# Four tokens a partition for x of batches 0 and 1, and a new order of the work up to the second chunk of w_in

## The chip, the cores and the metric

The kernel runs on one core of one Trainium2 chip. The metric is the time of one execution on the device, in microseconds (us). Four executions of the kernel before took 694.12, 694.25, 694.48 and 695.06 us; the median is 694.36. All data is float32, and the core's engines work side by side, each through its own list of instructions in program order: TensorE (PE, matmuls and transposes into PSUM banks), VectorE (DVE), ScalarE (ACT), GpSimd (POOL, hardly used here) and SyncE (SP), which issues all DMAs. They wait for each other through semaphores.

## What is computed

```python
# x (8, 8, 512, 64), state (8, 8, 32, 64): batches, heads, tokens or states, D
scores = scale * np.matmul(x, state.transpose(0, 1, 3, 2))
a = softmax(scores)                    # over the 32 states; max subtracted, 1e-9 added to the sum
xread = np.matmul(a, state)
scores2 = scale * np.matmul(state, x.transpose(0, 1, 3, 2))
a2 = softmax(scores2)                  # over the 512 tokens
sread = np.matmul(a2, x)
t = np.concatenate([xread, sread], axis=2)         # per head: 512 tokens, then 32 states
h = t.transpose(0, 2, 1, 3).reshape(8 * 544, 512) @ w_in      # w_in (512, 2048)
g = h * (1.0 / (1.0 + np.exp(-1.702 * h)))
out = g @ w_out                                     # w_out (2048, 512)
```

The inputs w_in and w_out arrive as 64-bit numbers and are turned into float32 on the core.

## The kernel before

The program is written out by hand: each engine runs its instructions in the order in which the Python code emits them (`manual_schedule`), so the order of the calls below is the order of each engine's queue. There is no planner and there are no due times.

**Weights.** w_in and w_out come as 32 pieces of 512 KB, 16 of w_in (four chunks `c` of 512 columns, four row blocks `k`) and 16 of w_out. Each is a DMA of SP (L199) and then three steps, called a piece's mask, clamps and rounding. `mask` (L221, DVE) takes the exponent bits. `round_a`, called by `powers_to`, clamps them with two Relu activations on ACT (L232, L233). `round_b`, called by `round_to`, is four DVE operations: `fraction` (L239), the sign (L250), the low word (L253) and the product (L257). `round_to(n, ahead)` finishes all pieces before n and, after each sign, has the masks and clamps of the next pieces done, `ahead` of them. The prologue's position of each such call sets where clamps stand in ACT's queue.

**Attention of batches 0 and 1, the prologue (L1188 to L1300).** `load_x` puts x into SBUF with 128 tokens a chunk, one per partition, in four DMAs a batch (L155), each run being one token of one head, 256 bytes. For later batches it already takes four tokens a partition, in runs of 1 KB (L152). `att_state` transposes the state of a batch and copies it on ACT into `pairs` (L308, block diagonal over two heads) and `stT` (L310). `xT_chunk` transposes one chunk of 128 tokens, four pairs of heads (L318), and copies it out on ACT (L319). `x_scores` makes the scores of one chunk for all heads (L325) in a PSUM bank that two chunks share. `head_max`, `head_sub`, `head_exp` and `head_norm` are the softmax over states (L338, L342, L346, L352 to L358), and `head_back` transposes the result (L367) and copies it to `aT` (L368). `att_scores` makes the second scores (L375) through `by_state`, one bank for each of two groups g of heads. Their softmax comes much later: `att_s_max` (L395), `att_s_exp` (L414), `att_s_norm` with `s_norm` (L420 to L423, where batches 0 and 1 scale the whole result), then `att_eT` (L509), `att_sread` (L523, L529) and `att_srT` (L537).

**The up projection of batches 0 and 1.** `att_M(b, c)` multiplies chunk c of w_in, all four row blocks, with the state (L375) and copies the two results M on ACT (L481). `up_x(b, f)` is two matmuls of M with aT (L552), followed by a Gelu on ACT (L555) into g_room; 16 of them per batch. `psH`, `att_ps` and the four `bank_o` are the eight PSUM banks; the last two of `bank_o` are `held`, and two banks of psH are `apart`. A matmul that reuses a bank waits until the engine that reads the old content is done. `keep_warm` issues matmuls of zeros.

**What follows.** The products with w_out for batch 0 (L1402) run piece by piece with the rounding of w_out and sums on DVE (L1332), interleaved with the rest of up_x of batch 1 (bank `down_up`). Then batch after batch runs through two levels of Strassen products (L695, L744, L1105), and a last pass for the state rows (L594). This part is not touched, apart from the order of rows in the stores of batches 0 and 1.

The order around the change, as it stands (L1200 to L1234), begins:

```python
    att_state(0)
    keep_warm(2, bank_o[0])
    xT_chunk(0, 0)
    keep_warm(2, bank_o[0])
    xT_chunk(0, 1)
    x_scores(0, 0, held)
    xT_chunk(0, 2)
    x_scores(0, 1, held)
    head_max(0, 0, held)
    mask(2)
```

Of the kernel before, what the change touches and what calls it, by code (L numbers as in the profile page):

```python
# [20 lines left out]
def kernel(  # L21
# [50 lines left out]
    out_x = out.rearrange("(b t) n -> b t n", b=B)[:, :S].rearrange("b (c q) n -> b c q n", c=SCH)  # L72
    out_s = out.rearrange("(b t) n -> b t n", b=B)[:, S:]
    x_v = x.rearrange("b h (c q) d -> b c q h d", c=SCH)
# [42 lines left out]
    pairs = konst.tile([P, NPR, NG, Ns], FP32, name="pairs")  # L117
# [17 lines left out]
    xn, xsq, stn = {}, {}, {}  # L135

    def load_state(b):
        stn[b] = apool.tile([P, NG, D], FP32, tag="stn", name=f"stn_{b}", bufs=2)
        for g in range(NG):
            nc.sync.dma_start(stn[b][:, g], st_v[b, g])  # L140

    def load_x(b):
        if b == 1:
            xn[b] = sums[:, 0].rearrange("p (c h d) -> p c h d", c=SCH, h=H)
        else:
            xn[b] = xpool.tile([P, SCH, H, D], FP32, tag="xn", name=f"xn_{b}")
        if b > 1:

            xn[b] = xn[b].rearrange("p c h d -> p (c h d)").rearrange("p (h c d) -> p h c d", h=H, c=SCH)
            for i in range(NG):  # L150
                h = slice(NPR * i, NPR * (i + 1))
                nc.sync.dma_start(xn[b][:, h].rearrange("p h c d -> p h (c d)"), x_four[b, :, h])  # L152
            return
        for c in range(SCH):
            nc.sync.dma_start(xn[b][:, c], x_v[b, c])  # L155
# [16 lines left out]
    def x_heads(b, c, j):  # L172
        return xn[b][:, c, NG * j : NG * (j + 1)].rearrange("q g d -> q (g d)")
# [7 lines left out]
    raw, power, begun = {}, {}, {}  # L181
# [59 lines left out]

    def round_b(i, ahead, follows):


        if i not in begun:
            fraction(i)
        dst = begun.pop(i)
        lo, hi = words(i)
        sc = power.pop(i)
        nc.vector.scalar_tensor_tensor(sc, hi, -0x80000000, sc, ALU.bitwise_and, ALU.bitwise_or)  # L250
        powers_to(ahead)

        nc.vector.scalar_tensor_tensor(dst, lo, 2.0**-32, dst.bitcast(I32), ALU.mult, ALU.add)  # L253
        del raw[i]
        if follows and i + 1 in raw:
            fraction(i + 1)
        nc.vector.scalar_tensor_tensor(dst, dst, 2.0**-20, sc.bitcast(FP32), ALU.mult, ALU.mult)  # L257
# [43 lines left out]
    def att_state(b):  # L301
        ps = att_ps([P, P], f"stT_{b}")
        nc.tensor.transpose(ps, stn[b].rearrange("p g d -> p (g d)"), ident)
        if b < 2:

            for g in range(NG):
                rows = slice(D * g, D * (g + 1))
                nc.scalar.copy(pairs[rows, :, g], ps[rows].rearrange("p (j n) -> p j n", n=Ns))  # L308
        A[b]["stT"] = apool.tile([P, P], FP32, tag="stT", name=f"stT_{b}", bufs=2)
        nc.scalar.copy(A[b]["stT"], ps)  # L310

    def xT_chunk(b, c):

        if c == 0:
            A[b]["xT"] = apool.tile([P, NPR, S], FP32, tag="xT", name=f"xT_{b}")
        ps = att_ps([P, NPR, P], f"xT_{b}_{c}")
        for j in range(NPR):
            nc.tensor.transpose(ps[:, j], x_heads(b, c, j), ident)  # L318
        nc.scalar.copy(A[b]["xT"][:, :, P * c : P * (c + 1)], ps)  # L319

    def x_scores(b, c, banks):

        ps = banks[c // 2].rearrange("p (c g j n) -> p c g j n", c=2, g=NG, j=NPR)[:, c % 2]
        for j in range(NPR):
            nc.tensor.matmul(ps[:, :, j], A[b]["xT"][:, j, P * c : P * (c + 1)], pairs[:, j], start=True, stop=True)  # L325

    def head_views(b, i, banks):
        a = A[b]
        if "mx" not in a:
            a["e1"] = apool.tile([P, SCH, NG, NPR, Ns], FP32, tag="e1", name=f"e1_{b}")  # L330
            a["mx"] = apool.tile([P, NG, NB], FP32, tag="mx", name=f"mx_{b}").rearrange("p g i -> p (g i)")
        n = NG * NB // 2
        t = a["e1"].rearrange("p c g j n -> p (c g j) n")[:, n * i : n * (i + 1)]
        return banks[i].rearrange("p (i n) -> p i n", n=Ns), t, a["mx"][:, n * i : n * (i + 1)]

    def head_max(b, i, banks):
        ps, _, mx = head_views(b, i, banks)
        nc.vector.reduce_max(out=mx, in_=ps, axis=AX.X)  # L338

    def head_sub(b, i, banks):  # L340
        ps, t, mx = head_views(b, i, banks)
        nc.vector.tensor_tensor(out=t, in0=ps, in1=mx.to_broadcast((P, NG * NB // 2, Ns)), op=ALU.subtract)  # L342
# [5 lines left out]
    def head_norm(b):  # L348

        t = A[b]["e1"]  # L350
        sm = apool.tile([P, NS1], FP32, tag="sm", name=f"sm_{b}")
        nc.vector.reduce_sum(out=sm, in_=t.rearrange("p c g j n -> p (c g j) n"), axis=AX.X)  # L352
        nc.vector.tensor_scalar(sm, sm, eps, None, ALU.add)
        nc.vector.reciprocal(out=sm, in_=sm)
        sm = sm.rearrange("p (c g j) -> p c g j", c=SCH, g=NG)
        for g in range(NG):
            e = t[:, :, g]
            nc.vector.tensor_tensor(out=e, in0=e, in1=sm[:, :, g].to_broadcast((P, SCH, NPR, Ns)), op=ALU.mult)  # L358

    def head_back(b, g):  # L360

        a = A[b]
        if g == 0:
            a["aT"] = low[:, :NG] if b == 1 else apool.tile([P, NG, S], FP32, tag="aT", name=f"aT_{b}")
        ps = att_ps([P, SCH, P], f"aT_{b}_{g}")
        for c in range(SCH):
            nc.tensor.transpose(ps[:, c], a["e1"][:, c, g].rearrange("p j n -> p (j n)"), ident)  # L367
        nc.scalar.copy(a["aT"][:, g], ps.rearrange("p c q -> p (c q)"))  # L368
# [8 lines left out]
    def att_scores(b):  # L377
        a = A[b]
        a["s"] = bank_o[:NG] if b == 0 else bank_o[NG:]
        by_state(b, a["s"], lambda rows, j: a["xT"][rows, j])  # L380

    def att_blocks(b):

        a = A[b]
        t = apool.tile([P, NG, NB, Ns], FP32, tag="e1", name=f"e1_{b}")
        a["e1"] = t
        for g in range(NG):
            nc.vector.transpose(t[:, g].rearrange("p i n -> p (i n)"), a["s"][g])

# [27 lines left out]
    def s_norm(b, g):  # L417

        e, sm = A[b]["e2"][g]
        nc.vector.tensor_scalar(sm, sm, eps, None, ALU.add)  # L420
        nc.vector.reciprocal(out=sm, in_=sm)
        if b < 2:
            nc.vector.tensor_scalar(e, e, sm, None, ALU.mult)  # L423
# [88 lines left out]
    def att_sread(b):  # L512
# [3 lines left out]
        for g in range(NG):  # L516
            for c in range(SCH):
                for j in range(NPR):
                    st = slice(Ns * j, Ns * (j + 1))
                    e, v = a["eT"][:, g, c, st], xn[b][:, c, NG * j + g] if b < 2 else None  # L520
                    if b > 1:
                        e, v = a["eT"][:, g, j, Ns * c : Ns * (c + 1)], xn[b][:, NG * j + g, c]
                    nc.tensor.matmul(  # L523
                        ps[st, g], e, v,
                        start=(c == 0), stop=(c == SCH - 1),
                    )
        sr = apool.tile([P, P], FP32, tag="sr", name=f"sr_{b}", bufs=2)
        if b < 2:
            nc.scalar.copy(sr, ps.rearrange("p g d -> p (g d)"))  # L529
        else:  # L530
            for g in range(NG):
                nc.scalar.activation(out=sr[:, D * g : D * (g + 1)], in_=ps[:, g], func=AF.Copy, scale=a["e2"][g][1])
# [662 lines left out]
    keep_warm(16)  # L1195
# [6 lines left out]
    keep_warm(2, bank_o[0])  # L1202
    xT_chunk(0, 0)
    keep_warm(2, bank_o[0])
    xT_chunk(0, 1)
    x_scores(0, 0, held)
    xT_chunk(0, 2)
    x_scores(0, 1, held)
    head_max(0, 0, held)
    mask(2)  # L1210
    head_sub(0, 0, held)
    fraction(2)
    xT_chunk(0, 3)
    x_scores(0, 2, held)
    x_scores(0, 3, held)
    powers_to(3)
# [4 lines left out]
    xT_chunk(1, 0)  # L1221
    head_exp(0)
    xT_chunk(1, 1)
    x_scores(1, 0, apart)
    round_to(3, 0)
    mask(3)
    xT_chunk(1, 2)
    x_scores(1, 1, apart)
    powers_to(4)
    keep_warm(2, held[0])  # L1230
    xT_chunk(1, 3)
    head_norm(0)
    head_back(0, 0)
    x_scores(1, 2, apart)  # L1234
    head_back(0, 1)
    x_scores(1, 3, apart)
    keep_warm(3, held[0])
    round_to(NPR, 1)
    att_M(0, 0)
    mask(NPR + 1)  # L1240
    mask(NPR + 2)
# [6 lines left out]
    powers_to(NPR + 2)  # L1248
    up_x(0, 0, True)
    up_x(0, 1, True)  # L1250
    round_to(NPR + 1, 0)
    head_norm(1)
    up_x(0, 2)
    for g in range(NG):
        head_back(1, g)
    powers_to(NPR + 3)
    up_x(0, 3)

# [9 lines left out]
    for i in range(nper):  # L1268
        up_x(1, i, bank=held[i] if i < 2 else None)
        if i + 1 < nper:  # L1270
            round_to(done["b"] + 1, 2 if i == 0 else AHEAD)
    att_M(0, 1)
    att_scores(1)
    turn(0, 1, (1, 1), [1, 1, 1])
# [6 lines left out]
    att_s_max(0)  # L1281
    att_s_max(1)
# [8 lines left out]
    for b in (1, 0):  # L1291
        att_s_exp(b, room[:, NG * b : NG * (b + 1)])
    rounds(3)
    for b in (1, 0):
        att_s_norm(b)
# [25 lines left out]
    def out_of(b):  # L1321
        return lambda r, n: out_x[b, r, :, n].rearrange("r q n -> q r n")
# [264 lines left out]
```

## Time and profile before

One execution was profiled. Its numbers, with those that matter for what follows:

| | |
|---|---|
| median of four executions | 694.36 us |
| the profiled execution | 694.85 us |
| its span, from the first to the last instruction | 693.1 us |
| granted TensorE clock over the span | 0.998 |
| PE busy from 0 to 10, 10 to 20, 20 to 30, 30 to 40, 40 to 50 us | 8.57, 8.60, 9.72, 9.12, 8.95 us |
| DVE busy in the same stretches | 3.56, 7.41, 9.86, 8.99, 9.82 us |
| ACT busy in the same stretches | 5.49, 6.01, 7.78, 9.00, 8.29 us |
| first real transpose of x of batch 0 / of batch 1 | 8.37 / 17.13 us |
| first matmul of up_x | 27.27 us |
| SP's issues of x: batch 0 / batch 1 | 3.04 to 7.92 / 10.73 to 16.58 us |

A row of the timeline gives the start in us, the duration, the engine, the line, the operation, the tile written and the tiles read (`out<-in`), the shapes, how many instructions are merged (`xN`) and, in brackets, the idle time before it and what ended it. PE matmuls are pipelined and their ends are modelled, so the distance of two starts says more than a duration. A matmul of float32 data shows as two instructions. In a table of windows, the columns are busy time and number of instructions of PE, PE's weight loads (PEld), DVE, ACT and POOL, then PE's granted clock, the share of the DMA engines' time in use, and GB/s. The chain of waits is followed back from the last instruction to what released each step.

### The profile page before, as it was taken

The numbers are of one execution on the slowest core, as the hardware profiler recorded it, in microseconds if no ns is written. First come the engines' busy times: TensorE is split into PE (matmuls) and PEld (weight loads), VectorE is DVE, ScalarE is ACT, GpSimd is POOL, SyncE is SP. The second block draws the span as 40 slices with busy tenths as digits, with TensorE's granted clock in tenths as the row PEclk, the third lists the DMA queues.
The fourth block names the chain that finished last, engine by engine and source line by source line (L and its number), as shares of the span: only waits on it lengthen the run. The fifth ranks groups of instructions, "written<-read, shape, count | busy, mean of one in ns | idle before, by whom it ended". The sixth has DMA issues, their size and how long they took to land.

```text
span 693.1 us, 13666 instructions
## 1 busy us (share of the span) xinstructions
PE 682.5 (98%) x5376; PEld 583.5 (84%) x5377; DVE 560.6 (81%) x1074; ACT 324.0 (47%) x712; POOL 1.0 (0%) x9
## 2 busy tenths in 40 slices
PE   8999999999999999999999999999999999999996
PEld 4533587778999899889988999989988998999995
DVE  5999998999999887788969796888688895886540
ACT  5887843224346533753365435643366236421410
POOL 0000000000000000000000000000000000000000
PEclk9999999999999999999999999999999999999999
DMA  8921338056443564347441845166424740251001
GB/s 223 384 97 54 102 122 185 7 192 208 159 91 111 176 197 138 59 137 201 138 93 49 234 160 122 24 185 204 119 42 141 210 139 16 76 168 46 3 1 30
DMA packets 106320, 87.41 MB, mean 126 GB/s; under 512 B 64784, under 2 KB 85776, under 8 KB 106256
## 3 DMA queue, kind: packets, MB, share of 16 engines
q1 hardware_dynamic: 106256, 86.53, 42.9%
q8 instruction: 43, 0.70, 0.4%
q14 instruction: 21, 0.17, 0.1%
HBM read 68.94 MB, written 17.56 MB: 125 GB/s over the span
## 4 chain that ended last, share of the span: by engine, by line
PE 92%; ACT 2%; DMA 2%; DVE 1%; SPq 1%; issue 0%; DVEq 0%
PE low L695 28%; PE o L1105 15%; PE o L695 15%; PE upx L1105 6%; PE h L552 4%; PE o L1402 4%; PE M L375 4%; PE down L1402 3%; PE o L594 2%; PE upw L1105 2%; PE o L744 2%; PE down_up L552 2%; PE sr L523 1%; PE upx_sr L1105 1%; DMA out_dram<-osb_sr 1%; PE o L375 1%
## 5 line engine op out<-in xcount | busy, mean ns | idle before, releaser
L695 PE MATMUL low<-w_out,g_room 128*128 128x128 f32 x416 | 54.3, 276 | 0.0
L695 PEld LDWEIGHTS low<-w_out,g_room 128*128 128x128 f32 x416 | 50.5, 192 | 4.5 <-issue 4.2
L1105 PE MATMUL o<-ta,M 128*128 128x256 f32 x192 | 49.9, 382 | 0.0
L1105 PE MATMUL upx<-aT,M 128*128 128x256 f32 x192 | 49.3, 379 | 0.0
L695 PE MATMUL low<-low,g_room 128*128 128x128 f32 x336 | 43.3, 275 | 0.0
L1105 PEld LDWEIGHTS o<-ta,M 128*128 128x128 f32 x192 | 35.5, 190 | 6.0 <-ACT g_room L1151 1.6
L695 PEld LDWEIGHTS low<-low,g_room 128*128 128x128 f32 x336 | 40.3, 192 | 0.0
L1105 PEld LDWEIGHTS upx<-aT,M 128*128 128x128 f32 x192 | 36.0, 190 | 4.6
L481 ACT COPY M<-M 128x512 f32<-128x512 f32 x57 | 29.7, 594 | 15.8 <-PE M L375 15.8
L1111 ACT ACTIVATE g_room<-o 128x512 f32<-128x512 f32 (+1 forms) x56 | 31.3, 560 | 10.4 <-PE o L1105 10.4
L695 PE MATMUL low<-sums,later 128*128 128x128 f32 x272 | 34.9, 275 | 0.0
L695 PEld LDWEIGHTS low<-sums,later 128*128 128x128 f32 x272 | 32.7, 192 | 0.1
L751 DVE TENSOR_TENSOR g_room<-g_room 128x512 f32<-128x512 f32 x48 | 31.7, 684 | 0.2
L375 PE MATMUL M<-w_in,stT 64*32 64x512 f32 x456 | 31.3, 594 | 0.0
L1105 PE MATMUL o<-ta,ms 128*128 128x256 f32 x120 | 30.8, 379 | 0.0
L552 PE MATMUL h<-aT,M 128*128 128x512 f32 x64 | 28.9, 599 | 1.0 <-ACT M L481 1.0
L1151 ACT COPY g_room<-o 128x512 f32<-128x512 f32 (+1 forms) x28 | 15.6, 555 | 25.4 <-PE o L1105 25.4
L1111 ACT ACTIVATE g_room<-g_room 128x512 f32<-128x512 f32 (+1 forms) x28 | 16.8, 600 | 20.8 <-DVE g_room L1114 20.8
L552 PEld LDWEIGHTS h<-aT,M 128*128 128x128 f32 x64 | 11.8, 190 | 17.4 <-issue 11.7
L1105 PEld LDWEIGHTS o<-ta,ms 128*128 128x128 f32 x120 | 22.8, 190 | 3.1
L1105 PE MATMUL o<-aT,m 128*128 128x256 f32 x96 | 24.6, 379 | 0.0
L695 PEld LDWEIGHTS o<-w_out,g_room 128*128 128x128 f32 x160 | 19.4, 192 | 5.0 <-issue 5.0
(293 smaller groups left out, 1639.6 us busy)
## 6 DMA issues: line engine op xcount, KB each, us to landing
low<-low SPq DMA_DIRECT2D x108, 256.0 KB, 2.7
low<-low SPq DMA_DIRECT2D x11, 768.0 KB, 4.3
later<-in_moe_w_out_dram SPq DMA_DIRECT2D x16, 512.0 KB, 3.4
w_out<-in_moe_w_in_dram SPq DMA_DIRECT2D x12, 512.0 KB, 5.3
xsq<-in_x_dram SPq DMA_DIRECT2D x96, 64.0 KB, 2.3
xn<-in_x_dram SPq DMA_DIRECT2D x12, 512.0 KB, 4.6
out_dram<-osb SPq DMA_DIRECT2D x15, 256.0 KB, 2.2
out_dram<-later SPq DMA_DIRECT2D x14, 256.0 KB, 2.1
```

What stands on the lines that cost most here:

```text
L375: nc.tensor.matmul(ps[g][st], A[b]["stT"][rows, st], rhs(rows, j), start=True, stop=True)
L481: nc.scalar.copy(m[:, g], ps[g])
L523: nc.tensor.matmul(ps[st, g], e, v, start=(c == 0), stop=(c == SCH - 1),)
L552: nc.tensor.matmul(hps, lhs[i], rhs[i], start=(i == 0), stop=(i == n - 1))
L594: nc.tensor.matmul(ps[:, r], lhs[f][:, P * r : P * (r + 1)], rhs[:, f], start=(first and r == 0 and f == 0), stop=(f == HF - 1), skip_grou ...
L695: nc.tensor.matmul(ps, lhs[f], rhs[:, f], start=(first and f == 0), stop=(f == QF - 1), skip_group_check=True)
L744: nc.tensor.matmul(ps[:, r], lhs[f][:, P * r : P * (r + 1)], rhs[:, f], start=(r == 0 and f == 0), stop=(f == HF - 1), skip_group_check=True,)
L751: nc.vector.tensor_tensor(out=out, in0=x0, in1=x1, op=op)
L1105: nc.tensor.matmul(ps[:, k], lhs[i][:, o : o + P], rhs[i], start=(first and k == 0 and i == 0), stop=(i == n - 1), skip_group_check=True,)
L1111: nc.scalar.activation(out=dst, in_=src, func=AF.Gelu_apprx_sigmoid)
L1151: nc.scalar.copy(c12, Y(u))
L1402: nc.tensor.matmul(ps7[name][:, HN * r : HN * (r + 1)], lhs[:, P * r : P * (r + 1)], rhs, start=(i == 0 and r == 0), stop=(i == HF - 1), s ...
```

## The change

x of batches 0 and 1 is loaded as for the other batches, with tokens 4q to 4q+3 on partition q, in four DMAs a batch of two heads each and runs of 1 KB. The transposes now take two token positions of one head at a time instead of one token chunk of two heads, so the scores' right side `pairs` is block diagonal over token positions, and half of the state products need the state with its two groups swapped. That state is loaded a second time (`turned`), transposed and copied (`stT2`). The second scores of a group lie in halves of two banks; their maxima, exps and sums are taken per half and joined, and the scaling moves from VectorE's `s_norm` to ACT's copy in `att_sread`. `head_norm` is split in two and `sign` is taken out of `round_b`, so that the prologue can place them. The prologue gets a new order, and the rows of `out` of batches 0 and 1 are stored in the new order of tokens.

```diff
     def load_state(b):
         stn[b] = apool.tile([P, NG, D], FP32, tag="stn", name=f"stn_{b}", bufs=2)
+        if b < 2:
+            turned[b] = apool.tile([P, NG, D], FP32, tag="turned", name=f"turned_{b}", bufs=2)
         for g in range(NG):
             nc.sync.dma_start(stn[b][:, g], st_v[b, g])
+            if b < 2:
+                nc.sync.dma_start(turned[b][:, 1 - g], st_v[b, g])
     def load_x(b):
...
-        for c in range(SCH):
-            nc.sync.dma_start(xn[b][:, c], x_v[b, c])
+        n = NG if b < 2 else NPR
+        for i in range(H // n):
+            h = slice(n * i, n * (i + 1))
+            nc.sync.dma_start(xn[b][:, h].rearrange("p h c d -> p h (c d)"), x_four[b, :, h])
...
+    def sign(i):
+        _, hi = words(i)
+        sc = signed[i] = power.pop(i)
+        nc.vector.scalar_tensor_tensor(sc, hi, -0x80000000, sc, ALU.bitwise_and, ALU.bitwise_or)
...
     def att_state(b):
-        ps = att_ps([P, P], f"stT_{b}")
+        ps = att_ps([P, P], f"stT_{b}") if b else bank_o[0][:, :P]
         nc.tensor.transpose(ps, stn[b].rearrange("p g d -> p (g d)"), ident)
...
+        ps2 = att_ps([P, P], f"stT2_{b}") if b else bank_o[1][:, :P]
+        nc.tensor.transpose(ps2, turned[b].rearrange("p g d -> p (g d)"), ident)
+        for i in range(2):
+            rows = slice(D * i, D * (i + 1))
             for g in range(NG):
+                src = (ps if g == i else ps2)[rows].rearrange("p (j n) -> p j n", n=Ns)
+                nc.scalar.copy(pairs[rows, :, g, i], src)
...
+    def state_copies(b):
+        for t, ps in zip(("stT", "stT2"), A[b]["turn"]):
+            nc.scalar.copy(A[b][t], ps)
+    def xT_part(b, j, bank=None):
...
+        for g in range(NG):
+            for i in range(2):
+                nc.tensor.transpose(ps[:, g, i], x_pair(b, NG * j + g, i), ident)
+        nc.scalar.copy(A[b]["xT"][:, h], ps)
+    def x_scores(b, j, banks):
+        ps = banks[j // 2].rearrange("p (c g j n) -> p c g j n", c=SCH, g=NG, n=Ns)[:, :, :, j % 2]
+        for g in range(NG):
+            for i in range(2):
+                nc.tensor.matmul(
+                    ps[:, 2 * i : 2 * i + 2, g], A[b]["xT"][:, NG * j + g, i], pairs[:, j, g].rearrange("p i n -> p (i n)"),
...
     def att_scores(b):
...
+        for g in range(NG):
+            for j in range(NPR):
+                st = slice(Ns * j, Ns * (j + 1))
+                for i in range(2):
+                    rows = slice(D * i, D * (i + 1))
+                    nc.tensor.matmul(
+                        a["s"][i][st, 2 * P * g : 2 * P * (g + 1)], a["stT" if g == i else "stT2"][rows, st],
+                        a["xT"][rows, NG * j + g], start=True, stop=True,
...
+    def two_s_max(b):
...
+        for i in range(2):
+            src = a["s"][i].rearrange("p (g t) -> p g t", g=NG)
+            nc.vector.tensor_reduce(out=mx[:, i], in_=src, axis=AX.X, op=ALU.max, negate=True)
+        nc.vector.tensor_tensor(out=mx[:, 0], in0=mx[:, 0], in1=mx[:, 1], op=ALU.min)
+        nc.vector.tensor_scalar(mx[:, 0], mx[:, 0], scale, None, ALU.mult)
+    def two_s_exp(b, room):
...
+        for g in range(NG):
+            dst = room[:, g].rearrange("p (k i q) -> p k i q", k=2, i=2)
+            for i in range(2):
+                nc.scalar.activation(
+                    out=dst[:, :, i], in_=a["s"][i][:, 2 * P * g : 2 * P * (g + 1)].rearrange("p (k q) -> p k q", k=2), func=AF.Exp,
+                    bias=a["mx2"][:, 0, g : g + 1], scale=scale, accum_out=sm[:, g, i : i + 1],
+                )
+    def two_s_norm(b):
...
+        nc.vector.scalar_tensor_tensor(sm[:, :, 0], sm[:, :, 0], eps, sm[:, :, 1], ALU.add, ALU.add)
+        nc.vector.reciprocal(out=sm[:, :, 0], in_=sm[:, :, 0])
...
-        if b < 2:
-            nc.vector.tensor_scalar(e, e, sm, None, ALU.mult)
...
-        if b < 2:
-            nc.scalar.copy(sr, ps.rearrange("p g d -> p (g d)"))
-        else:
-            for g in range(NG):
-                nc.scalar.activation(out=sr[:, D * g : D * (g + 1)], in_=ps[:, g], func=AF.Copy, scale=a["e2"][g][1])
+        for g in range(NG):
+            nc.scalar.activation(out=sr[:, D * g : D * (g + 1)], in_=ps[:, g], func=AF.Copy, scale=a["e2"][g][1])
```

The prologue's new order, from the warm-up on (the two calls of `keep_warm` further on write `held[0]`; the removed order is in the listing above):

```python
    keep_warm(14)
    powers_to(1); fraction(0); powers_to(2); round_to(2, 0)
    att_state(0)
    for j in range(NPR):
        keep_warm(1, held[0])
        xT_part(0, j, apart[j - 2] if j > 1 else None)
    for j in range(NPR):
        x_scores(0, j, held)
    mask(2); powers_to(3); state_copies(0)
    head_max(0, 0, held); head_sub(0, 0, held); fraction(2)
    head_max(0, 1, held); head_sub(0, 1, held)
    att_scores(0); att_state(1); state_copies(1)
    xT_part(1, 0); head_exp(0); keep_warm(1, held[0])
    xT_part(1, 1); x_scores(1, 0, apart)
    xT_part(1, 2); x_scores(1, 1, apart); keep_warm(1, held[0])
    xT_part(1, 3); x_scores(1, 2, apart)
    round_to(3, 1); head_sum(0); mask(NPR); powers_to(NPR + 1); head_scale(0)
    for g in range(NG):
        head_back(0, g)
    x_scores(1, 3, apart); keep_warm(2, held[0])
    round_to(NPR, 2); att_M(0, 0)
    # head_max, head_sub of batch 1 as before
    head_exp(1); att_M(1, 0, banks=held)
    up_x(0, 0, True); up_x(0, 1, True)
    fraction(NPR); sign(NPR); head_sum(1); head_scale(1); round_to(NPR + 1, 0)
    up_x(0, 2)
    for g in range(NG):
        head_back(1, g, held[g])
    powers_to(NPR + 3); up_x(0, 3); powers_to(NPR + 4)
    for i in range(nper):
        up_x(1, i, i < 2)
        if i + 1 < nper:
            round_to(done["b"] + 1, 2)     # before: ahead 2 only for i == 0, else 3
    att_M(0, 1); att_scores(1); powers_to(2 * NPR + 3)
```

Further on, `att_s_max`, `att_s_exp` and `att_s_norm` of batches 0 and 1 become `two_s_max`, `two_s_exp` and `two_s_norm` in the same places.

## The prediction

> **What bounds the kernel now.** I read the page first, then the chain of waits in order of time, then each engine's timeline up to 90 us.
>
> ```profile
> PE 682.5 (98%) x5376; PEld 583.5 (84%) x5377; DVE 560.6 (81%) x1074; ACT 324.0 (47%) x712; POOL 1.0 (0%) x9
> PE 92%; ACT 2%; DMA 2%; DVE 1%; SPq 1%; issue 0%; DVEq 0%
> ```
>
> TensorE is the bound, so time can only be won where PE does not yet run without a break. The chain in order of time shows where that ends:
>
> ```profile
> 10.73 6.26 DMA sums<-in_x_dram
> 16.99 0.14 issue
> 17.13 0.64 PE xT L318 x4
> ...
> 45.70 0.48 ACT M L481
> 46.23 5.42 PE h L552 x12
> 51.65 1.02 PE M L375 x16
> ```
>
> Up to 46.23 the chain changes engine dozens of times; from there it is PE almost to the end. PE's timeline shows what it waited for on the way:
>
> ```profile
> 27.27 5.42 PE L552 MATMUL h<-aT,M 128*128 128x512 f32 x12
> 33.57 1.14 PE L367 MATMUL aT<-ident,e 128*128 128x128 f32 x8 [0.88 <-ACT g_room L555]
> ...
> 46.23 5.42 PE L552 MATMUL h<-aT,M 128*128 128x512 f32 x12 [1.05 <-ACT M L481]
> ```
>
> Matmuls have a drain, so I count starts. Three up_x cost 3 x 1.715 = 5.15 from 27.27 (the chain has x16 of L552 in 7.06, 1.76 each with a wait; x4 in 1.72), so PE was free at 32.42 and stood until 33.57: 1.15. The second stop ends at 46.23 and began at about 45.0 (44.12 plus 0.9): 1.2. Both are ACT being late. The work up to that point is 17.5 us of PE.
>
> **The loads.** Of 256-byte runs the windows show 168 to 232 GB/s, of 1 KB runs (x of batch 3) 358 to 384:
>
> ```profile
> 6.00:7.00 1.00, 1.00 (x4) 0.31 (x3) 0.43 (x1) 0.91 (x3) 0.00 (x0) 1.00 0.83 168
> 7.00:8.00 1.00, 1.00 (x6) 0.43 (x4) 0.93 (x2) 0.97 (x3) 0.00 (x0) 1.00 1.02 213
> ...
> 161.00:162.00 1.00, 1.00 (x6) 0.90 (x5) 0.86 (x4) 0.98 (x2) 0.00 (x0) 1.00 1.09 384
> 162.00:163.00 1.00, 1.00 (x7) 0.87 (x6) 0.97 (x2) 0.99 (x2) 0.00 (x0) 1.00 1.06 358
> ```
>
> SP gains two state issues a batch (0.55 to 0.75 each, so 1.2 us), but an x issue of fewer runs falls from 1.03 (median, batch 0) to about 0.45 (L152). Bytes: 951 KB have moved at 5.0 us, weight pieces 0 and 1 are 1049 KB, done at 5.25; the doubled state (131 KB at 190) 5.94; each x quarter (262 KB at 380) 0.69, the last at 8.70. A piece was seen 1.08 after its bytes were in (3.9, seen 4.98), the first x chunk 1.5 (6.8, seen 8.36); with a quarter of the runs I take 1.1: quarters at 7.7, 8.4, 9.1, 9.8 (up to 10.2 at the other end). Before, the last was used at 12.16. Batch 1's x lands at 13.8 to 15.9 by the same sums, not 17.13. Nothing waits for the weights behind it.
>
> **Batch 0.** ACT has its second pair of clamps until 8.47, as now, then four `pairs` copies instead of two plus stT (0.26 each): the first xT copy starts at 9.4 (9.07 now), then every 0.49. PE turns all four parts first (0.44 each, a warm matmul of 0.21 between, two fewer ahead), until 10.25; scores follow without a break, 0.85 each (L325 10.04 to 10.88): second 11.95, last 13.65, where now it is 14.45. DVE: max and sub from 12.13, with fraction(2), 0.65 each: 15.2 (16.24 now). The clamps of piece 2 (1.45) and the two stT copies lie in ACT's idle time up to 13.6; if that is gone, att_scores(0) slips by the 0.5 of the copies. att_scores has 32 halves instead of 16, each of half the width: 0.95.
>
> **Batch 1.** att_state(1) ends at 14.85. ACT's four pairs and two stT copies run 15.05 to 16.6, and here is the new wait: xT_part(1, 0) takes the PSUM bank that the first stT copy frees, 16.36, and every transpose and score of batch 1 is queued behind it on PE. Transposes to 16.85, copy 17.05, exp(0) 17.55 to 18.6 (18.28 to 19.34 now). From there ACT is never free: parts of batch 1 until 21.4, clamps of pieces 3 and 4 (2 x 1.48) to 24.3, aT copies to 25.35, clamps of 5 to 26.75, M copies from 26.75. DVE: sum, mask(4), scale to 22.0, waits 0.55 for the clamps of 3 (new; pieces 3 and on are behind it), piece 3 at 25.1 as now. The first up_x starts with the first M copy at **27.35**, against 27.27. So all that was won in loads, some 0.75 us, is spent on ACT's extra copies and on clamps pulled ahead.
>
> What then changes is the two stops. The clamps now ahead are not between exp(1) and Gelu: table load and Gelu start at 29.8 and 31.05 (31.63 and 32.92 now), and head_back(1) takes the held banks instead of those that Gelu must free. PE goes 27.35 + 5.15 + 0.9 + five up_x (8.6) = 42.0 without a stop. One piece's clamps fewer (1.45) stand ahead of M(0,1)'s copies: 43.1 instead of 45.6. PE has M and att_scores (0.9 + 0.95) until 43.85, and its first copy is there at 43.65. **up_x(0,4) starts at 43.85, 2.4 earlier.** DVE must have piece 7 by 42.0: its own sum gives 41.3 (42.75 now).
>
> **Up to 86 us.** PE stays ahead by 2.4; pieces 11, 15 and 17 had 6 to 7 us in hand and keep at least 4. Then ACT becomes the bound once more:
>
> ```profile
> 74.82 0.69 ACT L414 ACTIVATE e<-o,mx 128x512 f32<-128x512 f32 x1
> 75.39 0.21 ACT L414 ACTIVATION_READ_ACCUMULATOR e<-o,mx 128x1 f32 x1
> 75.62 1.28 ACT L555 ACT_TABLE_LOAD   x1
> ...
> 84.22 0.27 ACT L529 COPY sr<-sr 128x128 f32<-128x128 f32 x1 [0.60 <-PE sr L523]
> ```
>
> Four exps with sums (every 0.66) become eight of half width. Not in the trace; bounds: 8 x 0.33 = 2.65, nothing more than now, and 8 x 0.66, 2.65 more. A copy of 512 takes 0.59, of 256 0.36 to 0.37, so 0.43 is nearest: **0.8** more. sr has two scaled copies a batch (0.31, every 0.27) for one of 0.27: 0.55 more. Against these stands the 0.60 that ACT waited at 84.22. M(1,3) needs the bank of the last sr copy: 0.75 of the 2.4 is lost, **1.7** stays. DVE loses four scalings of 0.40 and two adds/reciprocals (3.1 to 0.75), gains 0.35 in the maxima, and reaches T1 by the read of sums at 80.75, not 83.19: it stays ahead of PE.
>
> **At nothing.** Later tokens' order in `out` keeps 1 KB runs; the stores of batch 0 and 1 have no reader, and a store 1 us late would be hidden by the 20 us from the first one (143.64) to the next write of osb (163.60). The doubled memset of pairs (0.31 more on POOL before `edge`) ends before 2.2, needed at 5.51. sread and srT keep their matmul counts. DVE's later waits, with PE 2.1 us behind its sums at 131, shift along, since it gains 2.4.
>
> Sum: -1.15 - 1.2 (both stops) + 0.1 (start) - 0.15 (small gaps, as from 43.14 to 43.23) = -2.4; + 0.75 = **-1.65**, taken as -1.7. Span 693.1 to 691.4; with the 1.75 around it the profiled execution goes from 694.85 to 693.15. That execution lies 0.5 above the median 694.36, so the median forecast is **692.7**.
>
> **Rivals.**
> 1. ACT does not bind at 84 (exps at 0.33, slack taken): the whole 2.4 and up to 1 us more of the start (if batch 1's copies hide): 692.0 to 691.0. For it: ACT is 47% busy; against: 8 to 9 tenths from 30 to 60 and no gap from 71.53 to 82.7.
> 2. The exps cost 0.66 each: 1.85 more is lost, 692.7 + 1.85 = 694.5. For it: a fixed part is seen in the 0.2 reads; against: 0.36 for a copy of 256.
> 3. x lands no sooner: queued behind a doubled state, last quarter at 12.0, scores to 15.9, start at 29.6; the gain falls by 2.25 to -0.55: 694.9. It decides from a last quarter later than 11.5. Against it: 384 GB/s.
> 4. **Slower**: the array stays at half speed after the warm-up, in the place from 7.1 to 13 us. The rows: weight loads of the warm-up come every 0.43 until 6.71 and the next at 7.11, while the two warm matmuls of L132 from 7.65 need 0.59 with drain, so 0.21 each. The first 5.9 us ran at half speed. With 14 instead of 16, PE is done at 7.1, at the very switch, then has gaps while it waits for x. If another 5.9 us runs at half speed, 2.95 is lost: -1.7 + 2.95 = +1.25: 695.6, and above 695.75 with the first quarter 0.2 late too. It decides if transposes after 7.1 take 0.21 instead of 0.11.
>
> [...]
>
> **How the numbers follow.** Forecast 54% (its own range 691.7 to 693.7), rival 1 19%, rival 2 7%, rival 3 10%, rival 4 10%. What a measurement can tell from no change is about 0.2%, 1.39 us: faster is below 692.97, slower above 695.75. Of the forecast 36 points lie below 692.97, 18 above; rival 1 is faster with 19: faster 55%. Same: 18 + 4 + 8 = 30%. Slower: 3 points of rival 2 (if the sr copies slip as well), 2 of 3, 10 of 4: 15%. The range goes from 690.4 (rival 1 with 0.6 of DVE's idle time) to 695.4.
>
> **What would show it.** Right: the first L375 of M(0,0) near 25 and up_x at 27.3, no stop near 33 or 45, up_x(0,4) near 43.9, M(1,3) near 82.4 to 83.8, the eight exps 3.5 us. Wrong: x's first transpose after 8.5; up_x after 28.5; a PE stop between 86 and 145, which would mean that DVE, not PE, sets the pace of the pieces; transposes twice as long after 7.1.

## The result: slightly slower, and the profile after

The changed kernel took 695.71 us (median of 35 executions, 694.95 to 705.9), the kernel before, beside it, 694.48 (54 executions, 694.04 to 697.07): ratio **1.0020, interval 1.0012 to 1.0028**. The prediction said 692.7, faster. The highest time, 705.9, is the one execution in the chip's slower state (granted clock 0.982), and the ratio leaves it out. The profiled execution took 696.75, which is 1.0 above its own median; its span is 695.0, against 693.1 before.

TensorE (PE) still bounds the kernel, as the page's busy times and shares of the chain show:

```profile
PE 683.6 (98%) x5407; PEld 584.4 (84%) x5408; DVE 558.2 (80%) x1066; ACT 326.1 (47%) x728; POOL 1.2 (0%) x9
...
PE 94%; ACT 3%; DMA 2%; SPq 1%; DVE 0%; issue 0%; DVEq 0%
```

The chain of waits of the changed kernel, in order of time (start, duration, what), shows where its beginning went:

```profile
4.20 1.72 SPq L152
...
6.99 5.66 DMA xn<-in_x_dram
...
13.41 3.52 PE o L344 x32
...
30.31 5.35 PE h L608 x12
```

The start is now an issue of SP that stands 1.72 us, and the landing of x of batch 0. The first up_x, which started at 27.27 before, starts at 30.24. PE's timeline:

```profile
8.97 0.66 PE L336 MATMUL xT<-ident,xn 128*128 128x128 f32 x4
...
9.71 0.65 PE L336 MATMUL xT<-ident,xn 128*128 128x128 f32 x4
...
10.80 0.66 PE L336 MATMUL apart<-ident,xn 128*128 128x128 f32 x4 [0.22 <-DMA xn<-in_x_dram]
...
12.79 0.63 PE L336 MATMUL apart<-ident,xn 128*128 128x128 f32 x4 [1.12 <-DMA xn<-in_x_dram]
13.25 3.68 PE L344 MATMUL o<-pairs,xT 128*128 128x64 f32 x32
...
30.24 5.42 PE L608 MATMUL h<-aT,M 128*128 128x512 f32 x12
35.49 1.04 PE L389 MATMUL o<-ident,e 128*128 128x128 f32 x8
36.37 1.88 PE L608 MATMUL h<-aT,M 128*128 128x512 f32 x4
38.08 7.03 PE L608 MATMUL h<-low,M 128*128 128x512 f32 x16
45.04 1.09 PE L397 MATMUL M<-w_in,stT 64*32 64x512 f32 x16
45.93 1.07 PE L411 MATMUL o<-xT,stT 64*32 64x256 f32 x32
46.93 5.42 PE L608 MATMUL h<-aT,M 128*128 128x512 f32 x12
...
85.38 1.51 PE L397 MATMUL M<-w_in,stT 64*32 64x512 f32 x16 [0.21 <-ACT sr L588]
86.81 1.13 PE L1460 MATMUL o<-t_room,s_room 128*128 128x256 f32 x4
```

The kernel before had its last transposes of x of batch 0, and the product that is the last row above, at these times:

```profile
12.16 0.60 PE L318 MATMUL xT<-ident,xn 128*128 128x128 f32 x4
...
85.56 1.13 PE L1402 MATMUL o<-t_room,s_room 128*128 128x256 f32 x4
```

Three things are to be read here. The quarters of x are transposed at 8.97, 9.71, 10.80 and **12.79**, where the prediction had 7.7, 8.4, 9.1 and 9.8. Between the first up_x, up_x(0,0), and the fifth of batch 0, up_x(0,4) at 46.93, PE no longer stops: 16.69 us, against 46.23 - 27.27 = 18.96 before; so both stops are gone, as predicted. And the last row, the product P6 right behind M(1,3), comes 1.25 later than before, while up_x(0,4) came 0.70 later: between the two another 0.55 was lost.

### The profile page after: what moved, and what is told of

Its sections match the earlier page's. It is cut to its first block, busy times and chain, and to the rows that moved or that the text cites. A ratio compares the mean times of both kernels' runs of the same rounds, so it can differ in the third digit from the quotient of the medians.

```text
span 695.0 us, 13737 instructions
## 1 busy us (share of the span) xinstructions
PE 683.6 (98%) x5407; PEld 584.4 (84%) x5408; DVE 558.2 (80%) x1066; ACT 326.1 (47%) x728; POOL 1.2 (0%) x9
## 4 chain that ended last, share of the span: by engine, by line
PE 94%; ACT 3%; DMA 2%; SPq 1%; DVE 0%; issue 0%; DVEq 0%
PE low L751 28%; PE o L1161 15%; PE o L751 15%; PE upx L1161 6%; PE h L608 5%; PE M L397 4%; PE o L1460 4%; PE down L1460 3%; PE o L650 2%; PE upw L1161 2%; PE o L800 2%; PE down_up L608 2%; PE o L397 1%; PE upx_sr L1161 1%; DMA out_dram<-osb_sr 1%; PE sr L582 1%
## 5 line engine op out<-in xcount | busy, mean ns | idle before, releaser
L540 ACT COPY M<-M 128x512 f32<-128x512 f32 x57 | 29.6, 595 | 15.3 <-PE M L397 15.3
L608 PEld LDWEIGHTS h<-aT,M 128*128 128x128 f32 x64 | 11.8, 190 | 15.8 <-issue 11.5
```

The lines of the kernel that those rows point to most:

```text
L540: nc.scalar.copy(m[:, g], ps[g])
L608: nc.tensor.matmul(hps, lhs[i], rhs[i], start=(i == 0), stop=(i == n - 1))
```

## The experiments

Each run has executions of the kernel before beside it, on the same chip (medians 694.4 to 694.9); run 11 is a single execution. Runs 1 to 4, runs 5 to 8 with 11, and runs 9 and 10 are on three different chips. The ratios are against the kernel before on the same chip, so differences of a few tenths between runs on different chips are read from the profiles' rows and not from the medians. All build on the changed kernel unless said otherwise.

**1. One state load in place of two.** `turned` is not loaded; two matmuls of the two halves of `stn` with the identity give the swapped transpose.

```diff
...
-                nc.sync.dma_start(turned[b][:, 1 - g], st_v[b, g])
...
-        nc.tensor.transpose(ps2, turned[b].rearrange("p g d -> p (g d)"), ident)
+        for i in range(2):
+            nc.tensor.matmul(ps2[D * i : D * (i + 1)], stn[b][:, 1 - i], ident, start=True, stop=True)
```

> The changed kernel, but the swapped state is not loaded a second time; it comes from two small matmuls of the first state's halves with the identity. Theory A (the four small state loads stand ahead of x on SP and in the DMA rings, 512 packets of 256 bytes at some 135 per half us, and so x of batch 0 comes late): the last quarter of x is used some 1.1 us or more before 12.8 us, up_x starts near 29 instead of 30.2, total 694.3 to 694.9. Rival B (quarters in 1 KB runs are late by themselves, one slow ring): last quarter still used after 12.3, total within 0.4 of 695.7. Rival C (ScalarE's longer queue sets the start): first quarter sooner, up_x still near 30, total within 0.4 of 695.7.

Measured: **694.05**, ratio 0.9982 (0.9969 to 0.9995), where the changed kernel had 1.0020; the medians lie 1.66 apart. PE's timeline:

```profile
10.31 0.63 PE L333 MATMUL apart<-ident,xn 128*128 128x128 f32 x4
10.77 3.68 PE L341 MATMUL o<-pairs,xT 128*128 128x64 f32 x32
...
27.98 2.41 PE L605 MATMUL h<-aT,M 128*128 128x512 f32 x5
```

PE's rows show no wait for batch 0's x any more, and up_x starts 2.26 earlier than in the changed kernel. SP's timeline, first of the changed kernel, then of this one, with the issues of batch 0:

```profile
1.66 0.75 SPq L142 DMA_DIRECT2D stn<-in_state_dram  x1
2.45 0.55 SPq L144 DMA_DIRECT2D turned<-in_state_dram  x1
3.05 0.53 SPq L142 DMA_DIRECT2D stn<-in_state_dram  x1
3.62 0.53 SPq L144 DMA_DIRECT2D turned<-in_state_dram  x1
4.20 3.27 SPq L152 DMA_DIRECT2D xn<-in_x_dram  x4
```

```profile
1.65 1.34 SPq L140 DMA_DIRECT2D stn<-in_state_dram  x2
3.04 2.01 SPq L148 DMA_DIRECT2D xn<-in_x_dram  x4
```

x's issues start 1.16 earlier, as two state issues fewer should give, but end 2.42 earlier (5.05 against 7.47), because the first did not stand. The windows (granted clock, DMA share and GB/s are the last three columns) show what moved meanwhile; first the changed kernel, then run 1:

```profile
5.00:6.00 1.00, 1.00 (x4) 0.45 (x3) 0.51 (x2) 0.72 (x1) 0.00 (x0) 1.00 0.43 138
6.00:7.00 1.00, 1.00 (x4) 0.16 (x2) 0.58 (x2) 0.91 (x2) 0.00 (x0) 1.00 0.55 122
```

```profile
5.00:6.00 1.00, 1.00 (x5) 0.44 (x4) 0.69 (x2) 0.55 (x1) 0.00 (x0) 1.00 1.03 341
6.00:7.00 1.00, 0.39 (x2) 0.00 (x0) 0.43 (x1) 0.91 (x3) 0.00 (x0) 1.00 1.10 295
```

With the doubled state the DMA engines are half idle from 5 to 7 us: until x's first packet at 6.57 there is little but state packets for them. The packets of the trace, counted per 0.5 us, say at what pace: the state's 256-byte packets come at 126 to 139 per 0.5 us, 512 of them from 5.1 to 7.5 us, while the kernel before moved packets of the same size, nearly all of them x's, at 310 to 525. A state load has 128 packets, a load of x there 1024. It is not the spacing of the issues that sets this pace: the four issues were over at 4.15, before the first of these packets, and in run 11 batch 1's state keeps 140, 137 and 123 per 0.5 us although one of its four issues took 1.30. What sets it, no run shows.

**2. Scores of the first two quarters ahead of the last quarter's transposes.**

```diff
-    for j in range(NPR):
-        keep_warm(1, held[0])
+    for j in range(3):
+        keep_warm(1, held[j // 2])
         xT_part(0, j, apart[j - 2] if j > 1 else None)
-    for j in range(NPR):
-        x_scores(0, j, held)
-    mask(2)
-    powers_to(3)
+    x_scores(0, 0, held)
+    x_scores(0, 1, held)
     state_copies(0)
     head_max(0, 0, held)
     head_sub(0, 0, held)
+    mask(2)
     fraction(2)
+    xT_part(0, 3, apart[1])
+    x_scores(0, 2, held)
+    x_scores(0, 3, held)
+    powers_to(3)
```

> The changed kernel, but scores of pairs 0 and 1 of batch 0 stand before the transposes of the last quarter, as the chunks did before the change, and VectorE's mask of piece 2 stands behind the first max and subtraction. The loads are as in the change. Theory A' (all four transposes stand ahead of all scores, so one late quarter delays 3.6 us of scores): the last score of batch 0 starts near 14.3 instead of 16.0, up_x near 28.7, total 694.0 to 694.6. Rival C (ScalarE's extra copies and the clamps pulled ahead set the start of up_x): scores come sooner but up_x stays after 29.7, total above 695.2.

Measured: 695.16, ratio 1.0004 (0.9989 to 1.002); the last quarter at 13.14, up_x at 28.85. PE's place in the chain moved as expected, 1.39 at up_x; the median lies 0.55 below the changed kernel's, less than the 1.1 to 1.7 expected, and its interval overlaps that of the changed kernel, so the times alone do not show the gain.

**3. Both.**

> Both edits: no second state load, and scores of pairs 0 and 1 before the last quarter's transposes. Theory A with A': the two gains overlap, since each shortens the wait for the last quarter: up_x near 28 or a little before, total 693.0 to 694.0, so faster than the kernel before by 0.5 to 1.5 us. Rival C: not below 694.8.

Measured: 693.91, ratio 0.9977 (0.9962 to 0.9991); up_x at 27.72. Beside run 1 that is 0.26 earlier at up_x and 0.14 in the median, which these times do not tell apart: with x there in time, the order has little left to hide.

**4. The kernel before, with each state load of batches 0 and 1 issued twice**, the second time into a tile that nothing reads.

```diff
+        if b < 2:
+            again = apool.tile([P, NG, D], FP32, tag="again", name=f"again_{b}", bufs=2)
...
+            if b < 2:
+                nc.sync.dma_start(again[:, 1 - g], st_v[b, g])
```

> The kernel before the change, with each state load of batches 0 and 1 issued twice, the second copy into a tile that nobody reads. Theory A: x of batch 0 lands about 1.1 us later, x of batch 1 about 1 to 2 us later (17.1 becomes 18.2 or more), and the start of up_x moves from 27.3 to 28.3 or more: total 695.2 to 696.5. Rival B or C: the four small loads cost nothing, 694.2 to 694.8.

Measured: **698.5**, ratio 1.0043 (1.0027 to 1.0059), up_x at 31.34, 4.07 later than before. Four small loads cost the kernel before even more than expected. Part of it is the clock: in this execution PE was granted half speed from 19.1 to 26.0 us, behind a wait for x of batch 1. But three of the twelve executions have a granted clock of 0.998 or 0.999 over the span, and they took 696.55, 697.46 and 697.96, against a median of 694.61 for the 28 such executions of the kernel before beside them: the loads cost 1.9 to 3.4 us without the clock.

**5. The ACT term: two exps a batch instead of four**, on top of run 3. Group 1's own maximum and the two groups' own sums are left out.

```diff
-        for g in range(NG):
-            for i in range(2):
-                nc.scalar.activation(out=dst[:, :, i], in_=a["s"][i][:, 2 * P * g : 2 * P * (g + 1)]..., ...)
+        for i in range(2):
+            nc.scalar.activation(out=dst[:, i], in_=a["s"][i].rearrange("p (g k q) -> p g k q", g=NG, k=2), ...)
```

> The version with one state load and the scores between (693.69 in its profiled execution), with the second softmax of batches 0 and 1 as two exps of 512 a batch in place of four of 256: left out are group 1's own maximum and the two groups' own sums (group 0's maximum and one joint sum are used for both). Theory: ACT's list from the table load to the last sr copy sets M(1,3), and the prediction's price of it was only mis-sized. Eight exps at 0.45 each become four at about 0.66, so ACT is 0.95 earlier, M(1,3) and P6 come 0.7 to 1.0 earlier than 84.32, and the time falls by as much, to about 693.0. Rival: DVE or PE sets that place (ACT waits 1.22 us for PE's M at 84.47); then P6 stays within 0.2 of 84.32 and the time within 0.3 of 693.9.

**6. The same term from its other end: scaling on DVE again, one sr copy a batch**, on top of run 3; nothing is left out.

```diff
+        for e, one in A[b]["e2"]:
+            nc.vector.tensor_scalar(e, e, one, None, ALU.mult)
...
+        if b < 2:
+            nc.scalar.copy(sr, ps.rearrange("p g d -> p (g d)"))
...
```

> The version with one state load and the scores between, with the second softmax scaled on DVE again (four scalings of 0.40 us) and sr copied once a batch on ACT (0.27 in place of two of 0.27). Theory that ACT sets M(1,3): ACT saves 0.5, P6 comes 0.4 to 0.6 earlier, the time falls to about 693.4, unless DVE's 1.6 more shows. Rival, DVE is as close behind there: T1 comes up to 1.6 later and the time rises, to 694.0 to 695.0.

Measured: 693.35 in run 5 (ratio 0.9976, 0.9965 to 0.9988) and **693.06** in run 6 (0.9979, 0.9970 to 0.9988). Run 3, on another chip, has 0.9977, so these ratios do not show a gain over it; the profiles' rows do. P6 comes at 84.01 and 83.97, against 84.32 in run 3: 0.31 and 0.35 earlier, so ACT does bind there, though 0.95 us of exps bought only a third of that. The stop ahead of M(1,3), in run 3 and then in run 6:

```profile
82.88 1.51 PE L394 MATMUL M<-w_in,stT 64*32 64x512 f32 x16 [0.22 <-ACT sr L585]
84.32 1.13 PE L1460 MATMUL o<-t_room,s_room 128*128 128x256 f32 x4
```

```profile
82.53 1.50 PE L394 MATMUL M<-w_in,stT 64*32 64x512 f32 x16
83.97 1.13 PE L1465 MATMUL o<-t_room,s_room 128*128 128x256 f32 x4
```

With one sr copy the stop is gone (the two lines are another kernel's numbering, the same product). Against the kernel before, PE's lead in run 3 falls from 1.82 (at up_x(0,4)) to 1.49 by 80 us and to 1.24 at P6; in run 5 only the second of these falls is left, in run 6 only the first. So in run 3 the exps cost PE 0.33 and the scaled sr copies 0.25. DVE's four scalings cost nothing that can be seen.

**7. State of batch 0 issued by ACT instead of SP.**

```diff
+            q = nc.sync if b else nc.scalar
-            nc.sync.dma_start(stn[b][:, g], st_v[b, g])
+            q.dma_start(stn[b][:, g], st_v[b, g])
...
-                nc.sync.dma_start(turned[b][:, 1 - g], st_v[b, g])
+                q.dma_start(turned[b][:, 1 - g], st_v[b, g])
```

> The changed kernel with batch 0's four state loads issued by ACT in place of SP; nothing else moved. If the state's four issues on SP (2.5 us) and the stall of the third x issue behind them make x late, the x issues start near 1.7, the quarters land at 8.2 to 10.3 as with one state load, up_x starts near 28.0 and the time is about 694.1. If the small packets themselves hold x up (they share the DMA engines with it whoever issues them), the last quarter stays after 11.5 and the time after 695.0.

Measured: **697.71**, ratio 1.0043 (1.0031 to 1.0056). Neither side: x's issues started at 1.65 and its last packet came at 10.6, against 12.3, but now the state was late, first transposed at 9.43 (7.80): hardly any of its packets came between 6.2 and 7.2, while x's did, and the last came at 9.0 instead of 7.5. And PE, which had waited for it, ran at half clock from 9.8 to 13.2. Up_x started at 31.29. The two transfers shared the DMA engines (DMA share 0.93 to 1.03 from 6 to 10 us) although two engines issued them, and the state is needed first.

**8. Batch 2's squares one round later**, on top of run 3 (for a loss further on, below).

```diff
         if i == HF // 2:
             load_state(2)
+        if i == HF // 2 + 1:
             load_x_squares(2)
```

> The version with one state load and the scores between, with the 16 loads of batch 2's x in squares issued one round of the products later, behind the next two weight pieces. Theory: in kernels that are ahead of the kernel before, DVE waits at about 119 for the weight piece behind these 16 issues, and that gives part of the lead back between 144 and 182. Then the lead at P6 (1.24) is kept to 182 where it fell to 0.95: the time falls by 0.3 to about 693.6, and PE shows no stop for osb at 144 to 147. Rival: the lead is lost to something else (the stores, contention), and the drift and the time stay: 693.9.

Measured: 693.81, ratio 0.9982 (0.9970 to 0.9993). In the profile the lead at P6 (1.45) is kept past 182 (1.44), as expected, but 0.18 is lost at 228 and again at 569, and the time is run 3's within 0.1.

**9. Runs 3, 6 and 8 together.**

> One state load, scores between, the second softmax of batches 0 and 1 scaled on DVE with one sr copy, and batch 2's squares one round later, in one kernel. If the gains add: the lead at P6 of 1.6 us (one state load, scores between, scaling on DVE) is kept past 182 where it fell to 1.35, and the time is about 692.8, 1.6 below the kernel before. Rival, what the squares' move saved is lost again further on (near 228 and 569, as in the run with that move alone): 693.1, no better than scaling on DVE without the move.

Measured: **693.08**, ratio 0.9980 (0.9971 to 0.9989). The profile shows the lead of 1.70 kept to the end; the median is that of run 6 (693.06). So it is faster than both kernels, than the kernel before by 0.2%, and moving the squares adds nothing that these times show.

**10 and 11. x of batch 0 in two loads of four heads**, else the changed kernel; the second time for a profile alone.

```diff
-        n = NG if b < 2 else NPR
+        n = NG if b == 1 else NPR
```

> The changed kernel with x of batch 0 in two loads of four heads in place of four of two: the first eight loads of SP are then two weight pieces, four states and all of x. SP's list has a wait on the ninth and tenth load, for the first and second to be done; in the changed kernel these are the third and fourth quarter of x, here they are weight pieces. If such waits held x up, the issues of x take 0.5 each and are done by 5.3, the second half lands by 11, up_x starts by 28.8 and the time is about 694.4. If it was the first x issue itself that stood 1.7 us, whatever comes behind it, it stands again until 5.9, the last x lands after 12, up_x starts at 29.5 to 30.5 and the time is 695.2 to 696.

> The kernel with x of batch 0 in halves, once more, for one profile: in the profile of the first run PE ran at half clock from 9.2 to 12.6 us, just where its transposes of x stand, so that it doesn't tell what the earlier landing is worth. If this execution keeps full clock there: x in two loads lands by 10.5, the last quarter is transposed at 11.0 to 11.6 and up_x starts at 28.6 to 29.2, if the landing was what held PE; if up_x starts after 29.8 at full clock, something else than x's landing sets the start.

Measured: 695.58, ratio 1.0016 (1.0008 to 1.0025). The first x issue stood again (1.48 of the 2.03 of both), so it isn't the waits further down SP's list; yet the last x packet came at 10.3. In the first profile that bought nothing, and the windows' granted clock (third column from the end) says why:

```profile
8.00:9.00 1.00, 0.52 (x2) 0.15 (x2) 1.00 (x3) 0.99 (x5) 0.00 (x0) 1.00 1.08 381
9.00:10.00 1.00, 0.57 (x3) 0.57 (x4) 1.00 (x3) 0.12 (x1) 0.00 (x0) 0.62 1.10 369
10.00:11.00 1.00, 1.00 (x6) 0.74 (x5) 0.97 (x2) 0.41 (x1) 0.00 (x0) 0.50 1.07 394
11.00:12.00 1.00, 1.00 (x5) 0.79 (x5) 0.20 (x1) 0.30 (x2) 0.00 (x0) 0.50 1.05 418
12.00:13.00 1.00, 1.00 (x7) 0.86 (x6) 0.43 (x1) 0.47 (x2) 0.00 (x0) 0.68 0.78 299
```

PE ran at half speed for 3.41 us, from 9.2, and up_x started at 30.43 (696.63 us). The second profile, at full clock behind the warm-up (695.29 us):

```profile
11.62 0.60 PE L336 MATMUL apart<-ident,xn 128*128 128x128 f32 x4
12.05 3.68 PE L344 MATMUL o<-pairs,xT 128*128 128x64 f32 x32
...
29.04 5.42 PE L608 MATMUL h<-aT,M 128*128 128x512 f32 x12
```

The last quarter 1.17 earlier than in the changed kernel, up_x 1.20 earlier, the time 1.46 less than its profiled execution. The two executions of the same kernel lie 1.34 us apart, and their starts of up_x 1.39: that is what one stretch at half speed cost.

## Why the prediction was wrong

Its own sum, term by term, in the profiled executions (the rows of PE's starts against those of before):

| term | predicted | measured |
|---|---|---|
| the two stops and small gaps, up_x(0,0) to up_x(0,4) | -2.5 | -2.27 |
| start of up_x | +0.1 | **+2.97** |
| ACT at 72 to 84 | +0.75 | +0.55 |
| from 86 us on | 0 | +0.5 |
| sum | -1.65 | +1.75 |

The spans differ by 1.9; the other 0.15 stands behind the last matmul.

- **The step that failed is "The loads"**: "the doubled state (131 KB at 190) 5.94; each x quarter (262 KB at 380) 0.69, the last at 8.70". The last packet of x came at 12.26, 3.56 later: 0.63 of it is a late start of x's transfer and 2.93 a slow transfer.
  - The late start: the issues themselves were sized right (x's first at 3.04 + 1.2 = 4.24; it was 4.20), but that the first of them then stands 1.72 was not foreseen, and x's first packet came at 6.57 instead of 5.94. The state's packets ran beside it until 7.48: 131 KB in 2.4 us are 55 GB/s, by division, where 190 had been read from windows full of x's larger loads.
  - The slow transfer: x took 5.69 us from its first to its last packet, where the sum has 2.76. Its packets came at 140 to 174 per 0.5 us at best (380 GB/s would be 186), fell to 68 and 95 between 8.5 and 9.5, and the last 22 came one by one from 11.0 to 12.3. Even in run 1, with half the state loads, x took 4.8 us (4.83 to 9.62), in part beside the state and the next weight pieces; so a price for 380 GB/s without a break was too low by itself.
  - The 1.1 us from the last byte to its use was put too long (it was 0.53), which by luck hid 0.57 of the error. Run 1 gives back 2.26 of the 2.97, so most of it hangs on the second state load.
  - This is rival 3's mechanism with rival 3's point passed (12.79, "later than 11.5"), at a dearer price: it had the start at 29.6 and 694.9. Its counter-argument, 384 GB/s, was the wrong row.
- **From the landing to up_x(0,4) the sum was right.** From the last quarter's transposes to up_x the prediction has 27.35 - 9.8 = 17.55. Measured in that order of work: 17.45 (changed kernel), 17.67 (run 1), 17.42 (run 7), 17.42 (run 11). Only the point from which it counts was off, by 2.99 (12.79 for 9.8). From up_x to up_x(0,4) it has 16.5; measured 16.69 in the changed kernel and in runs 1, 3 and 11.
- **The stops went as argued**, and no new one took their place between 30 and 72 us. DVE's new wait for the clamps was sized right, 0.65 where 0.55 was put.
- **ACT at 72 to 84**: the eight exps take 3.76 against 2.78, +0.98 where +0.8 was put. The profile of the changed kernel, first and last of them:

```profile
73.51 0.47 ACT L441 ACTIVATE e<-o,mx 128x256 f32<-128x256 f32 x1
...
76.67 0.50 ACT L441 ACTIVATE e<-o,mx 128x256 f32<-128x256 f32 x1
...
84.79 0.95 ACT L588 ACTIVATE sr<-sr,sm 128x64 f32<-128x64 f32 x4
```

 PE paid less than ACT's sum, 0.55; runs 5 and 6 split run 3's loss there into 0.33 and 0.25. Rivals 1 and 2 are both wrong: ACT binds, and half an exp costs 0.45, between their 0.33 and 0.66.
- **From 86 us on** the prediction had nothing. In the profiled execution 0.5 was lost between 144 and 182. SP's timelines, of the kernel before and of the changed kernel, show an early link:

```profile
107.84 8.66 SPq L164 DMA_DIRECT2D xsq<-in_x_dram  x16
116.61 0.89 SPq L199 DMA_DIRECT2D later<-in_moe_w_out_dram  x2
```

```profile
109.09 10.18 SPq L161 DMA_DIRECT2D xsq<-in_x_dram  x16
119.37 0.91 SPq L196 DMA_DIRECT2D later<-in_moe_w_out_dram  x2
```

 The 16 issues took 10.18 us where they had taken 8.66, the next weight piece was issued at 119.37 (116.61 before), and DVE, waiting for it, went on at 123.13 (120.69 before), 2.4 behind where PE was 1.25 behind. With the squares moved (runs 8 and 9) that loss is gone from the profile. What makes the issues slower is open.
- **Rival 4**, the array at half speed: not in the profiled execution, whose clock record has full speed from 6.96 on, and not what sets the median: of the 35 executions 28 have a mean granted clock of 0.9975 or more, with a median of 695.59. That rival 4's 695.6 stands next to the measured 695.71 is a coincidence. But half speed did come in other profiles: in those of runs 4, 7 and 10 PE ran at it behind a wait, for 6.83, 3.4 and 3.41 us. Of the kernel before, beside runs 1 to 8, 15 of 62 executions lie below 0.9975, and took 695.37 to 699.51, so the kernel before has slower executions at a lower clock, which its first four times did not show (and none of 21 beside runs 9 and 10); of runs 1, 3, 5, 6, 8 and 9, whose x is there in time, none of 68.

Had x landed as in run 1, the sum would have come to 694.05: still 1.35 above 692.7, of which 0.6 is the start (27.98 for 27.35), and 0.8 was lost between 144 and 182 in its profile (an execution 0.5 above that median). So the forecast was too low even without its main error.

What stays open: why the first x issue stands (it did behind four state issues, in the changed kernel and in runs 2, 4, 10 and 11, and not in the runs with two; in the kernel before it is the second x issue that takes 2.2; in these six profiles the issue that stood ended between 5.64 and 5.92, and no run tests what it waited for), what sets the pace of the state's packets, and why single packets of x straggle, to 12.3 in the changed kernel and to 12.6 in run 2, and not in runs 1, 3, 10 and 11.

## What to carry to other kernels

Price a small load from rows of small loads, not by its bytes at the rate of larger ones: at the head of this kernel four loads of 32 KB in a row took 2.4 us, held the DMA engines half idle for 2 us, and the large load behind them, for which the critical path waited, came late. A copy that was needed in another arrangement came cheaper here from TensorE (two small matmuls, run 1, 1.66 us less in the median) than from a second load. And when a chain is worked out from one landing time, its error goes through: here 2.99 at the landing became 2.97 at the start of up_x. Bound that time from both sides before anything else.

## What the runs showed of the hardware that was not expected

- Four 32 KB loads with 256-byte packets moved at 126 to 139 packets per 0.5 us, and at 123 to 140 where one of their issues took 1.30 (run 11), while larger loads of packets of this size had moved at 310 to 525.
- Loads issued by ACT and by SP at the same time shared the DMA engines: x's last packet came at 10.6 instead of 12.3 and the state's at 9.0 instead of 7.5 (run 7).
- The granted clock fell early in the kernel, behind waits of PE: one stretch of 3.41 us at half speed in one of two profiles of the same kernel, 1.34 us in time (runs 10 and 11). Run 7's stretch is as long (9.8 to 13.2) and run 4's, 6.83 (19.1 to 26.0), is twice that. Counted in steps of 3.41 us, as run 10's stretch, from the first entry of the clock record, PE was busy for 0.48, 0.25 and 0.46 of the step before the fall in runs 10, 7 and 4; in the ten other profiles the emptiest step up to 680 us has 0.52, and none falls there. At the end of run 5 a step with 0.42, below run 4's 0.46, is not followed by a fall, so these shares give no threshold.
- x of batch 0 (1.05 MB in 1 KB packets) came faster in two loads than in four: 173 to 189 packets per 0.5 us in run 10 and 157 to 186 in run 11, against 140 to 174 in the changed kernel, each at best.
